# A fused attention and two-layer kernel: two PSUM banks given out as one place, and products of two steps at a time

## The chip, the cores and the metric

The kernel runs on one core of one Trainium2 chip. The metric is the device time of one execution in microseconds (us). The engines that matter are TensorE (matmuls, PE in the rows, with its weight loads as PEld), VectorE (DVE), ScalarE (ACT), GpSimd (POOL) and SyncE (SP), the last two used for issuing transfers here. Matmuls write to PSUM, which has eight banks of 512 fp32 columns for this kernel's purposes; VectorE and ScalarE read the results from there.

## What is computed

```python
def _attn_ref(x, state):                    # x (8,8,512,64), state (8,8,32,64)
    a = softmax(x @ state.T / 8);  xread = a @ state
    a2 = softmax(state @ x.T / 8); sread = a2 @ x
    return concatenate([xread, sread], axis=2)
def _moe_ref(x, w_a, w_b, w_out):           # 4352 rows, 512 -> 1536 -> 512
    return (x @ w_a) * (x @ w_b) @ w_out
def _moe2_ref(x, w_in, w_out):              # 512 -> 2048 -> 512
    h = x @ w_in
    return (h - tanh(h)) @ w_out
```

The three follow each other: attention, layer 1, layer 2. (The softmax subtracts the maximum and adds 1e-9 to the sum.)

## The kernel before

**Layer 1** goes over eight blocks of 512 tokens (blocks 0 to 7) and a block of the 256 state rows (block 8). A block has 12 steps f. In step f, `AB(blk, f)` makes two products a and b (twelve wide matmuls 128x512 of tile pab), VectorE and ScalarE form a times b in hi and lo parts (tile ph), and `X1(blk, f-1)` multiplies the step before by the output weights (twelve wide matmuls of tile acc). Every operand is kept as a hi and a lo part, and a product is made of three matmuls.

The attention read of a token block is not formed by itself: the states are multiplied with the weights first, and AB uses that product, tile mx. For blocks 0 and 1 this is `M(blk, f)`, one call a step: eight matmuls with outputs of 32x256 (16 records in the trace) into two tiles mp, one for each row half G. ScalarE writes the hi part from them; for block 0 a matmul by `minus` takes the hi part off in PSUM and ScalarE writes the lo part, for block 1 VectorE makes it. For blocks 2 to 7 it is `M_later(i, f, G)`: for blocks 2 to 5 (i = 0) 24 calls during block 1, each with twelve matmuls mq on two row tiles of 64 rows, one tile mq in PSUM for each; for blocks 6 and 7 (i = 1) 24 calls during blocks 4 and 5 on all 128 rows. These results go to memory and come back later.

Class `Att` does the attention of the next block beside that: scores (sc), transposes (pt, pl, pa), the state read (pr) and its transpose (pf). Block 0 has the attention of block 1 in it, part of its own, and also the decoding of the weights: 64-bit words come by DMA (rawab), ScalarE scales (line 116), and VectorE puts the words together in three steps (lines 119 to 121).

**PSUM before.** acc0 to acc3 are the four output tiles. In layer 1 `ab` gives out p2 and p3 in turn, and `att` gives out p0 and p1 in turn, one bank at a time, to everything else that is named above: sc, pt, pl, pa, pr, pf, mp, mq.

**Layer 2** has 64 slots with 512 tokens (`pair_slot`, eight blocks by eight slots) and eight slots with the 256 state rows (`plain_slot`). A pair slot forms the hidden layer for two feature groups from seven products of half the columns (B21, B11, T2, T3, T1, B22, T4, six narrow matmuls 128x256 each), which are added up in three tiles: y_ (py, bank p0, B21 only), x_ (px: B11, then T2, T1 and B22 on top; bank p1 in even slots and p3 in odd ones) and z_ (pz, bank p2: T3 and T4). ScalarE copies x_ after each of the four products (tile snap, lines 714, 727, 736, and h, line 748). VectorE adds the first copy to y_ (line 723, h1), others to z_ (h2). Between them stand the elementwise work of the slot before (lines 641 to 670: u, t, y, k, g) and the output matmuls acc of the slots before. In `plain_slot` a product `plain(s, g)` goes to bank p0 or p1 (g = 0, by the parity of s) or p2 or p3 (g = 1).

The order on each engine is made by the scheduler of the tile framework, which orders the instructions of the program by its own costs and puts in waits where tiles conflict. A tile is what it tracks: who reads and writes it, and when its place may be given to another tile.

## Time and profile before

| | us |
|---|---|
| median of three runs | 1451.9 |
| the three runs | 1450.9, 1451.9, 1454.3 |
| profiled execution | 1451.56 |
| its span | 1449.8 |
| TensorE busy in the span | 1427.9 (98%) |
| VectorE busy | 1129.5 (78%) |
| ScalarE busy | 904.8 (62%) |
| mean granted clock of TensorE | 0.999 |

The profile shows one execution. Busy time of an engine says how full it is, the chain that ended last says whose work set the end, and the timeline says when each instruction ran and what ended an idle time before it. Matmuls overlap: the busy time of one contains the tail in which the next is already running, so the cost of a row of matmuls is read from start to start.

### The profile page before, as it was taken

To read this page: it belongs to the slowest core of one execution; us is meant where nothing else is said; L and a number is where in the kernel's file an instruction comes from. 1 tells how busy PE (TensorE), PEld (TensorE's weight loads), DVE (VectorE), ACT (ScalarE), POOL (GpSimd) and SP (SyncE) were. 2 spreads that over 40 slices of the span, in tenths; PEclk is the share of its full clock that TensorE was granted. 3 is DMA by queue.
4 is the path that set the end of the run, shared out by engine and by line. 5 is a ranking of instruction groups with operands and counts; after the bars stand their busy time and mean duration, and the time that the engine had idled before them with its cause. 6 is when DMAs were issued, how large, how long until landed. Compare 5 with 4: busy or idle time off the path is not lost.

```text
span 1449.8 us, 23949 instructions
## 1 busy us (share of the span) xinstructions
PE 1427.9 (98%) x8928; PEld 1207.5 (83%) x8928; DVE 1129.5 (78%) x1984; ACT 904.8 (62%) x1752; POOL 207.9 (14%) x390
## 2 busy tenths in 40 slices
PE   5999999999999999999999999999999999999999
PEld 3666777878888878889988989899898998988998
DVE  6996656787544878772498988989899898988887
ACT  5765545565444556552467777777777867778675
POOL 0000001333111333320211110111101111011110
PEclk9999999999999999999999999999999999999999
DMA  8644337685546586853966667566665756656544
GB/s 297 234 144 144 130 125 220 209 265 180 163 121 183 171 255 221 249 180 126 318 195 204 197 189 224 171 205 195 204 208 174 226 171 207 204 186 211 160 146 127
DMA packets 103781, 280.50 MB, mean 193 GB/s; under 512 B 15216, under 2 KB 44400, under 8 KB 93936
## 3 DMA queue, kind: packets, MB, share of 16 engines
q0 software_dynamic: 41472, 178.28, 40.0%
q1 hardware_dynamic: 62192, 100.68, 21.2%
q8 instruction: 70, 1.15, 0.3%
q14 instruction: 47, 0.39, 0.1%
HBM read 216.53 MB, written 62.39 MB: 192 GB/s over the span
## 4 chain that ended last, share of the span: by engine, by line
PE 95%; DMA 2%; ACT 2%; DVE 1%; issue 0%; SPq 0%; ACTq 0%; DVEq 0%
PE acc L439 45%; PE pab L439 20%; PE px L630 13%; PE pz L630 6%; PE py L630 3%; PE mq L498 3%; DMA rawab<-in_wA 2%; PE mp L452 1%; PE pr L391 1%; PE sc L316 0%; PE pt L328 0%; ACT hab L116 0%; DMA x1d<-ev 0%; PE mp L460 0%; PE pa L328 0%
## 5 line engine op out<-in xcount | busy, mean ns | idle before, releaser
L439 PE MATMUL acc<-g,wo 128*128 128x512 f32 (+1 forms) x1728 | 436.1, 385 | 0.1
L439 PEld LDWEIGHTS acc<-g,wo 128*128 128x128 f32 x1728 | 293.4, 190 | 40.3 <-DVE g L670 0.3
L439 PE MATMUL acc<-ph,wo 128*128 128x512 f32 (+1 forms) x1296 | 307.7, 383 | 1.2 <-ACT ph L547 1.2
L439 PE MATMUL pab<-hl,mx 128*128 128x512 f32 x1152 | 294.7, 401 | 1.0 <-ACT hl L362 0.7
L439 PEld LDWEIGHTS acc<-ph,wo 128*128 128x128 f32 x1296 | 230.5, 188 | 53.9 <-issue 4.9
L439 PEld LDWEIGHTS pab<-hl,mx 128*128 128x128 f32 x1152 | 212.0, 189 | 62.0 <-issue 11.6
L545 DVE TENSOR_TENSOR ac<-ac,pab 128x512 f32<-128x512 f32 (+1 forms) x108 | 70.8, 656 | 142.3 <-PE pab L439 141.4
L257 POOL DMA_DIRECT2D wh<-whd x144 | 77.7, 539 | 670.3 <-PE pz L630 603.6
L665 ACT CAST g<-y 128x512 fp32r<-128x512 f32 (+1 forms) x144 | 86.0, 597 | 85.3 <-DVE y L661 84.3
L520 POOL DMA_DIRECT2D ml<-md x144 | 75.6, 526 | 421.5 <-DVE mx L526 247.5
L630 PEld LDWEIGHTS px<-T,wh 128*128 128x128 f32 x768 | 109.5, 190 | 11.0
L654 DVE SCALAR_TENSOR_TENSOR y<-y,u 128x512 f32<-128x512 f32 (+1 forms) x144 | 94.9, 659 | 26.8 <-ACT y L646 26.3
L630 PE MATMUL px<-B,wh 128*128 128x256 f32 x768 | 113.0, 283 | 1.4 <-ACT snap L736 1.4
L630 PE MATMUL pz<-T,wh 128*128 128x256 f32 x768 | 112.9, 283 | 0.0
L630 PE MATMUL px<-T,wh 128*128 128x256 f32 x768 | 112.8, 283 | 0.0
L630 PEld LDWEIGHTS px<-B,wh 128*128 128x128 f32 x768 | 105.4, 191 | 7.3 <-ACT snap L736 1.8
L542 ACT COPY ac<-pab 128x512 f32<-128x512 f32 (+1 forms) x108 | 60.7, 562 | 79.4 <-PE pab L439 79.2
L630 PEld LDWEIGHTS pz<-T,wh 128*128 128x128 f32 x768 | 105.5, 191 | 5.6
L661 DVE COPY_PREDICATED y<-k,t 128x512 f32<-128x512 int32 (+1 forms) x144 | 104.5, 726 | 2.8
L655 DVE SCALAR_TENSOR_TENSOR u<-t,u 128x512 f32<-128x512 f32 (+1 forms) x144 | 94.4, 656 | 9.0 <-ACT k L650 1.0
L670 DVE TENSOR_TENSOR g<-y,g 128x512 fp32r<-128x512 f32 (+1 forms) x144 | 94.4, 655 | 8.9 <-ACT g L665 8.8
L650 ACT ACTIVATE k<-u,consts 128x512 f32<-128x512 f32 (+1 forms) x144 | 99.8, 693 | 0.0
(233 smaller groups left out, 2089.7 us busy)
## 6 DMA issues: line engine op xcount, KB each, us to landing
wh<-whd POOLq DMA_DIRECT2D x64, 1024.0 KB, 5.3
wh<-whd POOLq DMA_DIRECT2D x72, 768.0 KB, 4.7
ml<-md POOLq DMA_DIRECT2D x144, 128.0 KB, 2.7
...
```

The lines of the kernel that those rows point to most:

```text
L257: nc.gpsimd.dma_start(t.rearrange("p a h c -> p a (h c)"), whd[j][:, a:b])
L439: nc.tensor.matmul(dst[:, cols], w[a], x[:, c, cols], start=first and i == 0, stop=last and i == 2)
L520: nc.gpsimd.dma_start(t[64 * G : 64 * G + 64, :], src[G, b])
L542: nc.scalar.copy(a[:, :n], pt[:, :n])
L545: at_v = nc.vector.tensor_tensor(a[:, :n], a[:, :n], pt[:, :n], ALU.mult)
L630: nc.tensor.matmul(dst, WP[s, piece][:, a, block(k)], XB[slots[s][0]][x][:, c, k, :], start=first and k == 0 and i == 0, stop=last and k = ...
L650: nc.scalar.activation(k, u, AF.Relu, bias=consts[:, 1:2], scale=1.0)
L654: nc.vector.scalar_tensor_tensor(y, y, PK, u, ALU.add, ALU.mult)
L655: nc.vector.scalar_tensor_tensor(u, t, C3, u, ALU.mult, ALU.mult)
L661: nc.vector.copy_predicated(y, k.bitcast(I32), t)
L665: nc.scalar.copy(GG[s, g][:, 0, : width(s)], EW[s, g][2])
L670: nc.vector.tensor_tensor(gt[:, 1, :n], EW.pop((s, g))[2], gt[:, 0, :n].bitcast(F32), ALU.subtract)
```

## The change

`att` is gone. Its two banks are one tag pp, one tile of 128 x 2 x 512, given out as a whole (`two_banks`) even where a user needs one bank (`one_bank`: pl, pa, pt, pr and pf, whose hunks are left out below). `scores` and `M` and `M_later` take both halves of one place. Attention stages are put together so that each place is emptied in the stage that fills it.

For block 1, `M_pair(blk, f)` makes steps f and f + 1 together: 16 small matmuls into two full banks, one ScalarE and one VectorE instruction of 512 columns for each row half. Its results lie in two tiles of 1024 columns, alternately in x4 and x5 and in the two mx places; a function in `MM` finds the part of a step.

In layer 2, `bank(i)` gives bank 0 and 1 as the halves of one tile PP that is taken once and kept to the end; banks 2 and 3 stay tiles of their own.

```diff
--- before.py
+++ after.py
@@ -76,7 +76,13 @@
     flat = lambda t: t.rearrange("p a b -> p (a b)")
 
 
-    att = Slots(abp, ["p0", "p1"])
+    def two_banks(name):
+
+        return abp.tile([128, 2, 512], F32, tag="pp", name=name)
+
+    def one_bank(name):
+        return two_banks(name)[:, 0]
+
     ab = Slots(abp, ["p2", "p3"])
     big = Slots(sp, [f"q{i}" for i in range(6)])
     small = Slots(sp, [f"r{i}" for i in range(8)])
@@ -187,7 +193,7 @@
                 VH[f // 2] = v_tile(f // 2, [128, 2, 1024], F32R, "wh")
             hi = VH[f // 2][:, f % 2]
         else:
-            hi = x_tile(f - 4, [128, 1024], "wh")
+            hi = x_tile(4 + (f - 6) % 4, [128, 1024], "wh")
         lo = (w_tile(2 * f - 2, [128, 1024], F32R, "wl") if f
               else big.get([128, 1024], F32R, "wl", LO0))
         nc.scalar.mul(hi, w, 2.0 ** -8)
@@ -308,8 +314,9 @@
 
         def scores(self):
 
+            sc = two_banks("sc")
             for G in range(2):
-                self.ps[G] = att.get([128, 512], F32, "sc")
+                self.ps[G] = sc[:, G]
             for p in range(KT):
                 for G in range(2):
                     r = slice(64 * G, 64 * G + 64)
...
@@ -410,15 +417,19 @@
 
             none = lambda: None
             yield none, none
-            yield none, (lambda: (self.scores(), self.load_xn()))
-            yield (lambda: (self.scale(0), self.scale(1), self.rows_max(0), self.cols_exp(0))), none
-            yield (lambda: self.cols_norm(0)), (lambda: self.turn(0))
-            yield (lambda: (self.rows_norm(0), self.turned(0))), none
+            yield none, (lambda: (self.scores(), self.load_xn(), self.scale(0), self.scale(1)))
+            yield (lambda: (self.rows_max(0), self.cols_exp(0))), none
+            if self.turned_by_pe:
+                yield (lambda: self.cols_norm(0)), none
+                yield (lambda: self.rows_norm(0)), (lambda: (self.turn(0), self.turned(0)))
+            else:
+                yield (lambda: self.cols_norm(0)), (lambda: self.turn(0))
+                yield (lambda: (self.rows_norm(0), self.turned(0))), none
             yield (lambda: (self.rows_max(1), self.cols_exp(1))), none
-            yield (lambda: self.cols_norm(1)), (lambda: self.turn(1))
-            yield (lambda: self.turned(1)), (lambda: self.sread())
-            yield (lambda: (self.sevac(), self.rows_norm(1))), (lambda: self.turn_s())
-            yield (lambda: self.keep_s()), none
+            yield (lambda: self.cols_norm(1)), (lambda: (self.turn(1), self.turned(1)))
+            yield none, (lambda: (self.sread(), self.sevac()))
+            yield (lambda: self.rows_norm(1)), (lambda: (self.turn_s(), self.keep_s()))
+            yield none, none
             yield none, none
             yield none, none
 
@@ -443,25 +454,52 @@
     minus = w_tile(23, [128, 128], F32R, "minus")
     nc.scalar.mul(minus, ident, -(2.0 ** 8))
 
+    def m_places(t):
+
+        m = t.rearrange("p a (g s c) -> p a g s c", g=2, s=2)
+        return lambda a, G, s: m[:, a, G, s, :]
+
     def M(blk, f):
 
-        mp = [att.get([128, 512], F32, "mp")[:, 0:256] for _ in range(2)]
+        both = two_banks("mp")
+        mp = [both[:, G, 0:256] for G in range(2)]
         for p in range(KT):
             for G in range(2):
                 r = slice(64 * G, 64 * G + 64)
                 nc.tensor.matmul(mp[G][32 * p : 32 * p + 32, :].rearrange("p (s c) -> p s c", s=2),
                                  STP[blk][r, 64 * p + 32 * G : 64 * p + 32 * G + 32], WA[f][r, :, p, :],
                                  start=True, stop=True)
-        m = MM[blk, f] = mix.get([128, 2, 512], F32R, "mx", *([] if blk == 0 else [MX]))
+        m = mix.get([128, 2, 512], F32R, "mx")
+        MM[blk, f] = m_places(m)
         for G in range(2):
             c = slice(256 * G, 256 * G + 256)
             nc.scalar.mul(m[:, 0, c], mp[G], 2.0 ** -8)
-            if blk == 0:
-                nc.tensor.matmul(mp[G], minus, m[:, 0, c], start=False, stop=True, skip_group_check=True)
-                nc.scalar.mul(m[:, 1, c], mp[G], 2.0 ** -8)
-            else:
-                nc.vector.scalar_tensor_tensor(m[:, 1, c], mp[G], 2.0 ** -8, m[:, 0, c].bitcast(F32),
-                                               ALU.mult, ALU.subtract)
+            nc.tensor.matmul(mp[G], minus, m[:, 0, c], start=False, stop=True, skip_group_check=True)
+            nc.scalar.mul(m[:, 1, c], mp[G], 2.0 ** -8)
+
+    def M_pair(blk, f):
+
+        both = two_banks("mp")
+        mp = [both[:, G] for G in range(2)]
+        for i in range(2):
+            for p in range(KT):
+                for G in range(2):
+                    r = slice(64 * G, 64 * G + 64)
+                    nc.tensor.matmul(
+                        mp[G][32 * p : 32 * p + 32, 256 * i : 256 * i + 256].rearrange("p (s c) -> p s c", s=2),
+                        STP[blk][r, 64 * p + 32 * G : 64 * p + 32 * G + 32], WA[f + i][r, :, p, :],
+                        start=True, stop=True, skip_group_check=True)
+        if f % 4 == 0:
+            hl = [x_tile(4 + i, [128, 1024], "mx") for i in range(2)]
+        else:
+            hl = [mix.get([128, 1024], F32R, "mx", [nm]) for nm in MX]
+        for G in range(2):
+            c = slice(512 * G, 512 * G + 512)
+            nc.scalar.mul(hl[0][:, c], mp[G], 2.0 ** -8)
+            nc.vector.scalar_tensor_tensor(hl[1][:, c], mp[G], 2.0 ** -8, hl[0][:, c].bitcast(F32),
+                                           ALU.mult, ALU.subtract)
+        for i in range(2):
+            MM[blk, f + i] = lambda a, G, s, i=i: hl[a][:, 512 * G + 256 * i + 128 * s : 512 * G + 256 * i + 128 * s + 128]
 
 
 
@@ -490,7 +528,8 @@
     def M_later(i, f, G):
         st = big.get([128, 2, 512], F32, "mst", RAW)
         tiles = [slice(0, 64), slice(64, 128)] if i == 0 else [slice(0, 128)]
-        mp = [att.get([128, 512], F32, "mq") for _ in tiles]
+        both = two_banks("mq")
+        mp = [both[:, r] for r in range(len(tiles))]
         for q in range(2):
             p = 2 * G + q
             for n, (a, c) in enumerate(hi_lo):
@@ -521,7 +560,7 @@
 
     def M_split(blk, f):
         t, m = MM[blk, f], mix.get([128, 2, 512], F32R, "mx", MX)
-        MM[blk, f] = m
+        MM[blk, f] = m_places(m)
         nc.scalar.copy(m[:, 0, :], t)
         nc.vector.tensor_tensor(m[:, 1, :], t, m[:, 0, :].bitcast(F32), ALU.subtract)
 
@@ -531,9 +570,9 @@
         for s in range(2):
             pt = ab.get([128, 512], F32, "pab")
             if blk < NB:
-                m = MM[blk, f].rearrange("p a (g s c) -> p a g s c", g=2, s=2)
+                m = MM[blk, f]
                 for G in range(2):
-                    product(pt, (m[:, 0, G, s, :], m[:, 1, G, s, :]), HL[blk][G], slice(0, n), G == 0, G == 1)
+                    product(pt, (m(0, G, s), m(1, G, s)), HL[blk][G], slice(0, n), G == 0, G == 1)
             else:
                 for k in range(KT):
                     product(pt, [w[:, s, k, :] for w in WH[f]], X0S[k], slice(0, n), k == 0, k == KT - 1)
@@ -691,7 +730,15 @@
             nc.scalar.copy(e, acc[m][:, :n])
         nc.sync.dma_start(outT[blk, m] if blk < NB else outS[m], e)
 
-    EV = [None]
+    EV, PP = [None], []
+
+    def bank(i, name):
+
+        if i < 2:
+            if not PP:
+                PP.append(two_banks("ph"))
+            return PP[0][:, i, half[0]]
+        return abp.tile([128, 512], F32, tag=f"p{i}", name=name)[:, half[0]]
 
     def OE(s, g, m):
         O(s, g, m)
@@ -700,8 +747,8 @@
     def pair_slot(s):
 
         blk, j = slots[s]
-        y_ = abp.tile([128, 512], F32, tag="p0", name="py")[:, half[0]]
-        x_ = abp.tile([128, 512], F32, tag=f"p{1 + 2 * (s % 2)}", name="px")[:, half[0]]
+        y_ = bank(0, "py")
+        x_ = bank(1 + 2 * (s % 2), "px")
         sn = mix.get([128, 3, 256], F32, "snap", SQ)
         h1, h2 = (mix.get([128, 512], F32, "h", [nm]) for nm in (mix.names[2], "ml2"))
         part(y_, s, 2, "B21", True, True)
@@ -725,7 +772,7 @@
             dve_rest(s - 1, 1)
         part(x_, s, 3, "T2", False, True)
         nc.scalar.copy(sn[:, 1], x_)
-        z_ = abp.tile([128, 512], F32, tag="p2" if s else "p0", name="pz")[:, half[0]]
+        z_ = bank(2 if s else 0, "pz")
         part(z_, s, 4, "T3", True, True)
         yield
         OE(s - 2, 1, 2)
@@ -760,7 +807,7 @@
 
     def plain(s, g):
         blk, j = slots[s]
-        t = abp.tile([128, 512], F32, tag=f"p{2 * g + s % 2}", name="ph_")[:, half[0]]
+        t = bank(2 * g + s % 2, "ph")
         x = XB[blk]
         for k in range(KT):
             w, xk = WP[s, (1, 2, 0, 7)[2 * g + k // 2]], x["B21" if k > 1 else "B11"]
@@ -826,12 +873,12 @@
             work()
 
     late0 = [
-        lambda A=A: (after_l1(lambda: (A.cols_exp(0), A.cols_norm(0))), A.turn(0)),
-        lambda A=A: (A.turned(0, tE[:, 0].rearrange("p (t s) -> p t s", s=128)),
-                     after_l1(lambda: (A.cols_exp(1), A.cols_norm(1))), A.turn(1)),
-        lambda A=A: (A.turned(1, tE[:, 1].rearrange("p (t s) -> p t s", s=128)), A.sread()),
-        lambda A=A: (A.sevac(), A.turn_s()),
-        lambda A=A: A.keep_s(),
+        lambda A=A: (after_l1(lambda: (A.cols_exp(0), A.cols_norm(0))), A.turn(0),
+                     A.turned(0, tE[:, 0].rearrange("p (t s) -> p t s", s=128))),
+        lambda A=A: (after_l1(lambda: (A.cols_exp(1), A.cols_norm(1))), A.turn(1),
+                     A.turned(1, tE[:, 1].rearrange("p (t s) -> p t s", s=128))),
+        lambda A=A: (A.sread(), A.sevac()),
+        lambda A=A: (A.turn_s(), A.keep_s()),
     ]
 
     for blk in range(NB):
@@ -892,12 +939,13 @@
                         X0S[k] = x
 
                 if nxt[0] < 2:
-                    M(*nxt)
+                    if nxt[1] % 2 == 0:
+                        M_pair(*nxt)
                 elif nxt[0] < NB:
                     M_split(*nxt)
                 AB(blk, f, bg=v, after=after)
             if blk == 0:
-                M(*nxt)
+                (M_pair if nxt[0] else M)(*nxt)
                 if f < len(late0):
                     late0[f]()
             if t and not blk:
```

TensorE, block 1, a step and a half with a group mp (M) and groups mq (M_later; wh and wl are hi and lo parts, sq the states), before:

```order
L452 MATMUL mp<-wa_457,stp 32x256 x8
L439 MATMUL pab<-hl,mx 128x512 x4
L439 MATMUL acc<-ph,wo_366 128x512 x2
L498 MATMUL mq<-wh,sq 128x256 x2
L498 MATMUL mq<-wl,sq 128x256
L498 MATMUL mq<-wh,sq 128x256 x2
L498 MATMUL mq<-wl,sq 128x256
L498 MATMUL mq<-wh,sq 128x256 x4
L498 MATMUL mq<-wl,sq 128x256 x2
L439 MATMUL acc<-ph,wo_366 128x512 x10
L498 MATMUL mq<-wh,sq 128x256 x4
```

and after, where mp stands for M_pair:

```order
L450 MATMUL acc<-ph,wo_298 128x512 x7
L488 MATMUL mp<-wa_358,stp 32x256 x8
L488 MATMUL mp<-wa_459,stp 32x256 x8
L450 MATMUL acc<-ph,wo_298 128x512 x5
L450 MATMUL pab<-hl,mx 128x512 x8
L537 MATMUL mq<-wh,sq 128x256 x4
L537 MATMUL mq<-wl,sq 128x256 x2
L537 MATMUL mq<-wh,sq 128x256 x4
L537 MATMUL mq<-wl,sq 128x256 x2
L450 MATMUL pab<-hl,mx 128x512 x4
```

The group of mq is no longer taken apart (x2, one, x2, one): its hi matmuls stand as x4, two row tiles in turn. Two steps of mp stand behind each other.

TensorE in a slot of layer 2, from B21 to T1 (py, px and pz are y_, x_ and z_), before:

```order
L630 MATMUL py<-B_8624,wh_9507 128x256 x6
L630 MATMUL px<-B_8257,wh_9507 128x256 x6
L439 MATMUL acc<-g,wo_10_6988 128x512 x6
L630 MATMUL px<-T_8862,wh_9507 128x256 x6
L630 MATMUL pz<-T_8980,wh_9507 128x256 x6
L439 MATMUL acc<-g,wo_10_6988 128x512 x3
L630 MATMUL px<-T_8743,wh_9509 128x256 x6
L439 MATMUL acc<-g,wo_10_6988 128x512 x3
L439 MATMUL acc<-g,wo_3_7002 128x512 x3
```

and after in an even slot (y_ and x_ are both ph):

```order
L669 MATMUL ph<-B_8520,wh_9627 128x256 x6
L669 MATMUL ph<-B_8157,wh_9627 128x256 x6
L450 MATMUL acc<-g,wo_12_7008 128x512 x6
L669 MATMUL pz<-T_8871,wh_9627 128x256 x6
L450 MATMUL acc<-g,wo_12_7008 128x512 x4
L669 MATMUL ph<-T_8755,wh_9627 128x256 x6
L450 MATMUL acc<-g,wo_12_7008 128x512 x2
L450 MATMUL acc<-g,wo_5_7022 128x512
L669 MATMUL ph<-T_8637,wh_9629 128x256 x6
```

T3 (pz) and four output matmuls have moved ahead of T2 (the first ph of T), which is the first to write x_ after the add of line 723 has y_ to read; T1 is the second ph of T.

VectorE in the last slots (y, u, t, k and g are the elementwise tiles; ph is the product), before:

```order
L659 SCALAR_TENSOR_TENSOR y<-y,u 128x256
L660 TENSOR_TENSOR t<-ph__15267,t 128x256
L661 COPY_PREDICATED y<-k,t 128x256
L654 SCALAR_TENSOR_TENSOR y<-y,u 128x256
L655 SCALAR_TENSOR_TENSOR u<-t,u 128x256
L670 TENSOR_TENSOR g<-y,g 128x256
L659 SCALAR_TENSOR_TENSOR y<-y,u 128x256
L660 TENSOR_TENSOR t<-ph__15314,t 128x256
L661 COPY_PREDICATED y<-k,t 128x256
L670 TENSOR_TENSOR g<-y,g 128x256
```

and after:

```order
L698 SCALAR_TENSOR_TENSOR y<-y,u 128x256
L699 TENSOR_TENSOR t<-ph,t 128x256
L700 COPY_PREDICATED y<-k,t 128x256
L699 TENSOR_TENSOR t<-ph,t 128x256
L700 COPY_PREDICATED y<-k,t 128x256
L709 TENSOR_TENSOR g<-y,g 128x256 x2
L693 SCALAR_TENSOR_TENSOR y<-y,u 128x256
L694 SCALAR_TENSOR_TENSOR u<-t,u 128x256
L698 SCALAR_TENSOR_TENSOR y<-y,u 128x256
L693 SCALAR_TENSOR_TENSOR y<-y,u 128x256
```

The work of two halves was interleaved, one t and one copy at a time; after, the two t and copies stand in a row, and the two g after them.

## Rows read from the trace of the kernel before

**Rows 1.** The page, part 4: the chain that ended last, by engine.

```profile
PE 95%; DMA 2%; ACT 2%; DVE 1%; issue 0%; SPq 0%; ACTq 0%; DVEq 0%
```

**Rows 2.** Busy time by stretch of 25 us (length, each engine, clock, DMA share, GB/s).

```profile
25.00:50.00 25.00, 23.83 (x208) 14.89 (x207) 23.70 (x40) 19.46 (x41) 0.00 (x0) 1.00 0.79 277
50.00:75.00 25.00, 23.62 (x141) 16.06 (x139) 22.46 (x38) 17.26 (x34) 0.00 (x0) 1.00 0.56 194
1000.00:1025.00 25.00, 25.00 (x158) 22.61 (x157) 23.61 (x42) 16.86 (x33) 2.69 (x5) 1.00 0.51 162
```

**Rows 3.** Timeline, TensorE, block 0 (start, busy us, instruction): M in halves and whole.

```profile
33.41 0.50 PE L439 MATMUL acc<-ph,wo 128*128 128x512 f32 x1
33.84 0.64 PE L452 MATMUL mp<-wa,stp 64*32 64x256 f32 x8
...
51.03 0.66 PE L452 MATMUL mp<-wa,stp 64*32 64x256 f32 x16
```

**Rows 4.** Timeline, TensorE, one slot of layer 2.

```profile
1073.06 0.88 PE L630 MATMUL px<-B,wh 128*128 128x256 f32 x6
1073.78 1.57 PE L439 MATMUL acc<-g,wo 128*128 128x512 f32 x6
1075.18 0.88 PE L630 MATMUL px<-T,wh 128*128 128x256 f32 x6
```

**Rows 5.** Timeline, TensorE, block 1: groups of M_later, and scores (132.11).

```profile
129.74 0.70 PE L498 MATMUL mq<-wh,sq 64*128 64x256 f32 x3
...
130.98 1.20 PE L439 MATMUL acc<-ph,wo 128*128 128x512 f32 x4
132.11 1.09 PE L316 MATMUL sc<-xTt,stp 64*32 64x512 f32 x16
...
205.64 0.50 PE L498 MATMUL mq<-wh,sq 64*128 64x256 f32 x4
...
206.32 0.28 PE L498 MATMUL mq<-wl,sq 64*128 64x256 f32 x2
206.52 1.65 PE L439 MATMUL acc<-ph,wo 128*128 128x512 f32 x6
```

**Rows 6.** Busy time from 112.8 to 231 us of line 498 (M_later) alone.

```profile
112.80:231.00 118.20, 27.65 (x288) 22.22 (x288) 1.00 0.46 148
```

**Rows 7.** Busy time from 112.8 to 231 us of line 452 (M) alone.

```profile
112.80:231.00 118.20, 9.96 (x192) 2.69 (x192) 1.00 0.46 148
```

**Rows 8.** Chain of waits, block 0 (start, us, piece): the words of the weights.

```profile
43.93 7.68 DMA rawab<-in_wA
...
51.63 1.17 ACT hab L116
```

**Rows 9.** Timeline, VectorE, block 0: the last step on the words of step 4.

```profile
46.12 1.22 DVE L121 SCALAR_TENSOR_TENSOR wa<-hab,wa 128x1024 int32<-128x1024 int32 x1
```

**Rows 10.** Timeline, TensorE, block 0: a correction by minus that waited.

```profile
54.16 0.39 PE L460 MATMUL mp<-mx,minus 128*128 128x256 f32 x1 [0.87 <-ACT mx L458]
```

**Rows 11.** Timeline, VectorE and ScalarE, same slot: the add for h1, a copy of x_.

```profile
1076.49 0.42 DVE L723 TENSOR_TENSOR h<-snap,py 128x256 f32<-128x256 f32 x1
...
1076.59 0.37 ACT L727 COPY snap<-px 128x256 f32<-128x256 f32 x1
```

**Rows 12.** Timeline, ScalarE, weight loads, TensorE: a wait in slot 1.

```profile
727.79 0.38 ACT L736 COPY snap<-px 128x256 f32<-128x256 f32 x1
...
728.22 0.78 PEld L630 LDWEIGHTS px<-B,wh 128*128 128x128 f32 x6 [1.82 <-ACT snap L736]
...
728.22 0.86 PE L630 MATMUL px<-B,wh 128*128 128x256 f32 x5 [1.39 <-ACT snap L736]
```

**Rows 13.** Timeline, VectorE, last slots.

```profile
1438.51 0.42 DVE L670 TENSOR_TENSOR g<-y,g 128x256 fp32r<-128x256 f32 x1 [0.47 <-ACT g L665]
...
1444.23 0.42 DVE L670 TENSOR_TENSOR g<-y,g 128x256 fp32r<-128x256 f32 x1 [0.47 <-ACT g L665]
```

10 lines of the change are left out of this document (5 added, 5 removed).

## The prediction, made before the changed kernel was run

> **What bounds the kernel now.** I read the chain of work that ended last first: TensorE holds 95% of it [rows 1]. So a change is worth what it takes from TensorE, or what it makes TensorE wait. The table by stage comes next [rows 2]. In block 0 (25 to 75 us) TensorE and VectorE are both nearly full, 23.83 and 23.70 of 25 us; in layer 2 TensorE leaves no gap and VectorE has 1.4 us of 25 to spare. The change touches three places: the small matmuls of blocks 0 and 1, the order inside a slot of layer 2, and the last eight slots.
>
> **Small matmuls in block 1.** Two prices matter. The first is the switch between wide and small matmuls: one wide matmul alone between two half groups takes 33.84 - 33.41 = 0.43 us [rows 3] where a row of them runs at 0.233 (1073.78 to 1075.18 is six, 1.40 us [rows 4]), so a way in and out costs 0.20 us. The second is the group itself. A half M and a whole M take nearly the same, 0.64 and 0.66 us [rows 3]: the halves run side by side only when they are issued together, so an M in halves costs about 0.57 more, and another switch. The same holds for the twelve matmuls of M_later: 1.24 us (129.74 to 130.98) from their start to the next wide one where the row tiles come one after the other, 0.88 (205.64 to 206.52) where they alternate [rows 5].
>
> By the order after, all 24 mq groups alternate (one is cut in two), and 12 M become six M_pair. Between 112.8 and 231 us the mq matmuls are busy 27.65 us and the M matmuls 9.96 [rows 6, 7]. An alternating group is busy 0.96 us (205.64 to 206.60 [rows 5]), so 24 make 23.0: 4.6 saved. For M_pair no row stands. From below it is bounded by the whole score group, with as many columns in all, 1.09 us [rows 5], from above by two whole M, 1.32 [rows 3]; I take 1.18, nearer to the score group, which has its shape, so six make 7.1: 2.9 saved. Counted in the timeline, 42 stretches of small matmuls stand between wide ones from 112.83 to 229.62; the order after has 36, and 6 x 0.20 is 1.2. Together 8.7. Busy times count the overlapping ends of matmuls too; the same sum made from intervals between starts is 45.8 us before and 37.8 after, so I take **8.0 us** saved. The evacuations that the pairs merge lie beside a full TensorE and count nothing.
>
> Against it stands the single place. With two banks given out one at a time a group could start while the one before was read; now it waits until all of that is evacuated. In the order after, 6 to 10 wide matmuls (1.4 to 2.3 us) stand between one mq group and the next, and emptying two banks is two or three instructions of 0.6 to 0.7 us on two engines, so most is covered; behind the state read and its transpose only two wide ones (0.47 us) stand ahead of the next mq. I take 1 us for such places (0 to 3): **-7.0 us**, -8 to -5.
>
> **Block 0.** Five of the M there are in halves before and none after; the scores come whole. By the same count of intervals from 22.5 to 112.8 us there are 25.4 us of small work before, and 18.9 by the order after: 6.5 less. How much of it shows is doubtful. The words of the weights come through a DMA of 7.7 us, ScalarE (1.17 us) and VectorE [rows 8], and over 25 to 75 VectorE is idle 3.8 us in all [rows 2]. On the other side, TensorE is behind there rather than ahead: M(0,4) starts at 51.03 [rows 3] and its last words were ready at 47.34 [rows 9]. And new waits appear: a whole M needs the place free from the scores, transposes and state read, and the correction by `minus` follows M at once in two places, where before one such cost 0.87 us of idle time behind ScalarE [rows 10]. I take about half, **-3.5 us** (-6.5 to 0).
>
> **Slots of layer 2.** Banks 0 and 1 are one tile there. In a slot with even number x_ lies in bank 1 and y_ in bank 0; T2 writes x_, and now waits for the VectorE add that forms h1 out of y_, though that reads the other bank. To hide it the scheduler has put T3 and four output matmuls ahead of T2. Counted from the start of the last B11 matmul (m0 = 1073.66, the sixth of those that start at 1073.06 and take 0.12 each): 0.12, six output matmuls 1.40 (1073.78 to 1075.18), T3 0.72 (as B11, 1073.06 to 1073.78), four output matmuls 0.93: T2 could start at m0 + 3.17 [rows 4]. The add is over at 1076.91 [rows 11], m0 + 3.25, and it stands in VectorE's queue behind work released before m0, so nothing brings it earlier. That is 0.08 us too late. To it comes what a wait itself costs TensorE: after its wait at 728.22 the weights are loaded 0.05 us after ScalarE ended (727.79 + 0.38), and five matmuls take as long as six in a row do, 0.86 against 0.88, so the first one costs 0.10 more [rows 4, 12]. So 0.23 us for T2. In the same slots T1 and B22 are covered by three output matmuls: 0.12 + 0.70 = 0.82 us, against 0.32 until the copy of x_ starts (estimated from its starts in the timeline), 0.37 for it [rows 11], 0.05 and 0.10: 0.02 us short each. 31 even slots x 0.27 = **+8.4 us**. Lowest 31 x 0.08 = 2.5 (the wait without its own cost), highest about 11.5 (the add 0.1 us later). Behind the waiting T2 all of TensorE's queue stands. Odd slots keep x_ in bank 3 and wait for nothing new.
>
> On PSUM the Trainium skill ("PSUM — Partial Sum Buffer", PSUM bank collisions raise a hardware error) says that engines working on different banks run clean and only a shared bank and quadrant collides. By that the chip itself would not need T2 to wait for the add, and without the wait layer 2 would lose nothing: 1442.9 us. The order with its waits shows that this program waits all the same, both banks being one tile, so I give that no more than 0.02.
>
> **The last eight slots.** The first half of a slot lies in bank 0 or 1 by parity. Because of the one tile VectorE and ScalarE take the elementwise work of two halves in pairs instead of in turn, and the next slot's first product waits for ScalarE's reading. In turn, a slot of VectorE's work takes TensorE's 5.72 us (1438.51 to 1444.23), with an idle spot of 0.47 us in it [rows 13]; the same instructions in pairs I add up to 5.85 to 5.9. So about 0.15 us a slot is lost once a slack of some 0.8 is used up, and at the end the last g comes about 1 us later with no product left to cover it. **+1.5 us** (0 to +4).
>
> **Sum.** -7.0 - 3.5 + 8.4 + 1.5 = -0.6 us. The profiled execution took 1451.56 us, 1.76 more than its span; the median is 1451.9, on which this gives **1451.3 us**: within the 0.2% (2.9 us) that a measurement can tell from no change.
>
> **Rivals.** (1) The even slots hardly wait: faster. If T2 costs only the 0.08 us by which the add is late, layer 2 loses 2.5 us and the time is 1445.4. For it: 0.08 is little, and an add 0.1 us earlier takes away all. Against it: the 0.15 us on top at 728.22. (2) The one place becomes the bound: slower. If each of some 30 hand-overs of blocks 0 and 1 leaves TensorE 0.25 us idle, because an evacuation queues behind ScalarE's 1.17 us pieces of the weights, 7.5 us go on top: 1458.8. It decides from about 0.12 us a hand-over on (+3.6 us, 1454.9). For it: both engines' queues in block 0 are full; against: 1.4 us and more of cover in block 1. (3) The change doesn't do what it says: the row tiles of a group don't run side by side when both write one tile. They would keep 1.24 us, 24 x 0.28 more than summed: 1458. The order shows them alternate into separate banks, as the group at 205.64 does, so little. (4) Block 0 gives all of its 6.5 us: 1448.3, faster.
>
> **How the numbers follow.** No change 0.41; faster 0.34 (rival 1 0.18, rival 4 and mixtures 0.14, no wait 0.02); slower 0.25 (rival 2 0.15, rival 3 0.02, the upper ends of the even slots and of the tail 0.08). 1444 to 1458 leaves out the outermost of rivals 1 and 2, about 0.1 on either side.
>
> **What would show it.** Small matmuls of block 1 in 36 stretches, mq at 0.88 us each, and block 2 some 10 us earlier than before. In layer 2 even slots of 10.9 us beside odd ones of 10.64, and T2's wait on h1 in the list of TensorE's waits, some 7 us over 31. If block 2 comes less than 6 us earlier, the hand-overs cost more than I took; if even slots take under 10.75 us, the wait is cheaper, and the kernel faster than forecast.

## The result

The changed kernel takes 1462.5 us (median of four runs, 1460.8 to 1463.1) where the kernel before takes 1452.9 on the same chip (1450.9 to 1454.3). The ratio is 1.007, with a 95% interval of 1.0056 to 1.0084: 9.6 us slower. The profiled execution took 1463.11 us, its span is 1461.3. The prediction was no change at 1451.3 us, with a range of 1444 to 1458.

The difference of the two spans is 11.5 us. It is laid out by stage below, from the starts of TensorE's matmuls in the timelines: the first wide one of AB(0,0), AB(1,0) and AB(2,1), the thirteenth (128x256 there) of AB(8,0), the start of T4 in slots 2 and 62, and the end. The columns before and after are those of the two profiled executions; the last holds the terms of the prediction's sum.

| stage | before | after | difference | predicted |
|---|---|---|---|---|
| to AB(0,0) | 21.28 | 21.61 | +0.33 | 0 |
| block 0 | 95.71 | 95.16 | -0.55 | -3.5 |
| block 1 | 116.38 | 113.93 | -2.45 | -7.0 |
| blocks 2 to 7 | 431.01 | 431.31 | +0.30 | 0 |
| block 8, slots 0 and 1 | 76.00 | 78.38 | +2.38 | 0 |
| slots 2 to 62 | 638.40 | 648.48 | +10.08 | +8.4 |
| the rest, with the last eight slots | 70.99 | 72.44 | +1.45 | +1.5 |

AB(2,1) starts 2.7 us earlier than before (230.70 for 233.37), where the prediction had named some 10, and less than 6 as the sign that the hand-overs cost more than it took.

The chain that ended last has changed, part 4 of the page of after (shares of the span):

```profile
PE 87%; DVE 6%; ACT 3%; DMA 2%; issue 1%; SPq 0%; DVEq 0%; ACTq 0%
```

TensorE held 95% of it before [rows 1] and holds 87% now; VectorE went from 1% to 6%. These are the waits in the list of TensorE's waits of after (line and tile that waited, what released it, us in total, times, longest) that are new or have grown:

```profile
PE mp L477 <- ACT mx L476: 3.8, 5, 1.4
...
PE px L669 <- ACT snap L783: 2.0, 1, 2.0
PE mq L537 <- ACT mst L542: 1.2, 3, 0.5
...
PE mp L488 <- DVE mst L544: 0.6, 2, 0.4
PE mq L537 <- DVE sm L380: 0.6, 1, 0.6
...
PE ph L669 <- DVE h L770: 0.4, 2, 0.2
```

The first is the correction by `minus` of block 0 (1.6 us in 3 before), the second slot 1 of layer 2 (1.4 before), the next three the groups of block 1. The last is T2 in the even slots of layer 2, and it has only two entries and 0.4 us, though the even slots are the largest loss of all. A slot shows why. TensorE in the even slot 34 of after (start, busy us, instruction):

```profile
1079.03 1.57 PE L450 MATMUL acc<-g,wo 128*128 128x512 f32 x6
1080.43 0.88 PE L669 MATMUL pz<-T,wh 128*128 128x256 f32 x6
1081.15 1.09 PE L450 MATMUL acc<-g,wo 128*128 128x512 f32 x4
1082.32 0.95 PE L669 MATMUL ph<-T,wh 128*128 128x256 f32 x6
1083.11 0.86 PE L450 MATMUL acc<-g,wo 128*128 128x512 f32 x3
```

Four wide output matmuls take 0.93 us [rows 4]; here T2 (ph<-T at 1082.32) starts 1.17 us after the first of them. The 0.24 us more are not idle in the profile, since the modelled end of the last wide matmul (1081.15 + 1.09 = 1082.24) covers most of them, and what is left is too short for the list. VectorE's add for h1, the weight loads of T2 and ScalarE's g in the same slot:

```profile
1081.76 0.41 DVE L770 TENSOR_TENSOR h<-snap,ph 128x256 f32<-128x256 f32 x1
...
1082.29 0.77 PEld L669 LDWEIGHTS ph<-T,wh 128*128 128x128 f32 x6 [0.47 <-ACT g L704]
...
1081.31 0.62 ACT L704 CAST g<-y 128x512 fp32r<-128x512 f32 x1 [1.01 <-DVE y L700]
```

The add ends at 1082.17, the weights are loaded from 1082.29. The view names ScalarE's g as what ended that wait, but g was done at 1081.93. Behind the add the weights follow by 0.12 us in every one of the 30 even slots from 4 to 62: T2 waits for the add, as the prediction had it. The same add stands in rows 11. The lengths of an odd and an even slot are read from T4 to T4, TensorE in after:

```profile
1086.45 0.88 PE L669 MATMUL pz<-T,wh 128*128 128x256 f32 x6
...
1097.07 0.88 PE L669 MATMUL pz<-T,wh 128*128 128x256 f32 x6
...
1108.07 0.88 PE L669 MATMUL pz<-T,wh 128*128 128x256 f32 x6
```

The odd slot takes 10.62 us and the even one 11.00; together 21.6, where two slots of before take 21.28.

### The profile page after: what moved, and what is told of

Read it like the earlier page. It is cut to its first block, busy times and chain, and to the rows that moved or that the text cites. A ratio compares the mean times of both kernels' runs of the same rounds, so it can differ in the third digit from the quotient of the medians.

```text
span 1461.3 us, 23987 instructions
## 1 busy us (share of the span) xinstructions
PE 1430.3 (98%) x8928; PEld 1191.9 (82%) x8928; DVE 1132.8 (78%) x1972; ACT 901.0 (62%) x1740; POOL 208.4 (14%) x390
## 4 chain that ended last, share of the span: by engine, by line
PE 87%; DVE 6%; ACT 3%; DMA 2%; issue 1%; SPq 0%; DVEq 0%; ACTq 0%
PE acc L450 41%; PE pab L450 19%; PE ph L669 10%; PE px L669 6%; PE pz L669 6%; PE mq L537 2%; DMA rawab<-in_wA 1%; DVE u L694 1%; DVE y L693 1%; DVE y L698 1%; PE pr L398 1%; DVE t L699 1%; DMA md<-mst 0%; DVE y L700 0%; PE pt L335 0%
## 5 line engine op out<-in xcount | busy, mean ns | idle before, releaser
L450 PE MATMUL acc<-g,wo 128*128 128x512 f32 (+1 forms) x1728 | 441.2, 385 | 0.5 <-ACT g L704 0.5
L450 PE MATMUL pab<-hl,mx 128*128 128x512 f32 x1152 | 297.7, 402 | 0.9 <-ACT hl L369 0.7
L263 POOL DMA_DIRECT2D wh<-whd x144 | 77.9, 541 | 683.0 <-PE pz L669 416.5
L693 DVE SCALAR_TENSOR_TENSOR y<-y,u 128x512 f32<-128x512 f32 (+1 forms) x144 | 94.9, 659 | 38.0 <-ACT y L685 38.0
L669 PEld LDWEIGHTS ph<-B,wh 128*128 128x128 f32 x768 | 102.6, 190 | 11.5 <-ACT snap L783 6.1
L669 PE MATMUL ph<-B,wh 128*128 128x256 f32 x768 | 108.3, 284 | 0.0
L685 ACT ACTIVATE y<-u,consts 128x512 f32<-128x512 f32 (+1 forms) x144 | 98.8, 686 | 0.7 <-DVE g L709 0.6
L698 DVE SCALAR_TENSOR_TENSOR y<-y,u 128x512 f32<-128x512 f32 (+1 forms) x144 | 95.0, 660 | 2.7
```

Source lines behind the costliest of these rows:

```text
L263: nc.gpsimd.dma_start(t.rearrange("p a h c -> p a (h c)"), whd[j][:, a:b])
L450: nc.tensor.matmul(dst[:, cols], w[a], x[:, c, cols], start=first and i == 0, stop=last and i == 2)
L669: nc.tensor.matmul(dst, WP[s, piece][:, a, block(k)], XB[slots[s][0]][x][:, c, k, :], start=first and k == 0 and i == 0, stop=last and k = ...
L685: nc.scalar.activation(y, u, AF.Square, bias=consts[:, 0:1], scale=1.0)
L693: nc.vector.scalar_tensor_tensor(y, y, PK, u, ALU.add, ALU.mult)
L698: nc.vector.scalar_tensor_tensor(y, y, PC, u, ALU.add, ALU.mult)
```

## The experiments

Each is compared with the kernel before on the same chip, whose medians were 1453.1, 1453.1, 1453.5 and 1452.9 us in four sets of runs. A table behind them has the stages of all profiles. Of the edits the deciding lines are shown; `...` marks what is left out.

### Layer 2 apart

y_ goes alone into a place that is taken anew each slot, x_ always into bank 3, and the last eight slots' first products into places of their own.

```diff
...
-            return PP[0][:, i, half[0]]
+            return one_bank(name)[:, half[0]]
...
-        y_ = bank(0, "py")
-        x_ = bank(1 + 2 * (s % 2), "px")
+        y_ = bank(0, "py") if s else first()[:, 0, half[0]]
+        x_ = bank(3, "px") if s else first()[:, 1, half[0]]
...
```

> The change with layer 1 as it is, but in layer 2 y_ alone in the place pp and x_ in bank 3 in every slot but slot 0, and the last slots' first product alone in pp: no tile there holds two things any more. Theory (the tie between the two banks costs layer 2 its loss): slots of 10.64 us again, even ones too, so about 10 us off the pair slots and 1.4 off the end: a span near 1449.8 us and a time of 1450 to 1452 us. Rival (the even slots grow for another reason, such as the order of ScalarE's work or where layer 1 leaves the transfers): even slots stay above 10.9 us and the time stays at 1459 or more.

Measured: 1450.5 us, ratio 0.9986 (0.9974 to 0.9997). Slots 2 to 62 take 638.40 us again, to the hundredth what they took before. So the tie of y_ and x_ is the whole loss of the pair slots; layer 1 of the change, still in this kernel, is worth a little. T4 in two slots that follow each other, T2 and the add:

```profile
1079.13 0.88 PE L669 MATMUL pz<-T,wh 128*128 128x256 f32 x6
...
1089.77 0.88 PE L669 MATMUL pz<-T,wh 128*128 128x256 f32 x6
...
1073.45 0.88 PE L669 MATMUL px<-T,wh 128*128 128x256 f32 x6
...
1074.77 0.40 DVE L773 TENSOR_TENSOR h<-snap,py 128x256 f32<-128x256 f32 x1
```

Here, as in the kernel before, T2 is over before the add begins (1074.33 and 1074.77), and while the add reads y_ (in the kernel before from 1076.49 to 1076.91 [rows 11]) TensorE goes on writing T3 and output matmuls into other banks, at no cost that shows. That agrees with the Trainium skill ("PSUM — Partial Sum Buffer", PSUM bank collisions raise a hardware error), which has accesses to different banks run clean. The wait was the program's, not the chip's.

### The last eight slots tied again

The same, but the first products of the last eight slots are again halves of one tile.

```diff
...
-        t = bank(2 * g + s % 2, "ph")
+        t = tied()[:, s % 2, half[0]] if g == 0 else bank(2 + s % 2, "ph")
```

> Layer 2 apart in the pair slots, but the first products of the last eight slots are again the halves of one tile, as in the change. Theory: the end alone costs 1 to 2 us, so 1451.5 to 1452.5 us where the run with all apart had 1450.5. Rival (the end costs nothing, TensorE has work to cover it): 1450 to 1451 us.

Measured: 1452.1 us, 1.5 more than the run with all apart (1450.5, in another set, in which the kernel before had the same median). That alone is not clear of the spread of these two sets (1449.8 to 1453.9, and 1447.4 to 1456.7). The profiles are clearer: the rest behind slot 62 takes 72.44 and 72.47 us in the two kernels that tie the last slots, and 70.98 to 71.55 in the twelve others, 71.42 in the run with all apart. VectorE's first g of a slot and TensorE's last output matmuls in the change show how:

```profile
1443.49 0.41 DVE L709 TENSOR_TENSOR g<-y,g 128x256 fp32r<-128x256 f32 x1
...
1449.33 0.42 DVE L709 TENSOR_TENSOR g<-y,g 128x256 fp32r<-128x256 f32 x1
...
1453.85 3.61 PE L450 MATMUL acc<-g,wo 128*128 128x256 f32 x24 [0.48 <-ACT g L704]
```

From 1443.49 to 1449.33 is 5.84 us, where a slot took 5.72 [rows 13]; and at 1453.85 TensorE has stood still for 0.48 us until ScalarE's g was there.

### Two tiles in layer 1

M_pair and the regrouped attention stages stay, but p0 and p1 are two tiles given out in turn, in both layers.

```diff
+    att = Slots(abp, ["p0", "p1"])
     def two_banks(name):
-        return abp.tile([128, 2, 512], F32, tag="pp", name=name)
+        return [att.get([128, 512], F32, name) for _ in range(2)]
     def one_bank(name):
-        return two_banks(name)[:, 0]
+        return att.get([128, 512], F32, name)
...
-        both = two_banks("mq")
-        mp = [both[:, r] for r in range(len(tiles))]
+        mp = [one_bank("mq") for _ in tiles]
...
```

> The change with M_pair and the regrouped attention stages, but p0 and p1 as two tiles given out in turn, in layer 1 and in layer 2. Theory (in layer 1 the gain was lost because the two banks of one tile are emptied one after the other): the copies of a group of M_later on ScalarE and VectorE may start together again, the waits of TensorE in block 1 (about 4.4 us beyond the switches) mostly go, although some groups fall apart into unpaired ones; the second AB of block 2 begins 5 to 6 us earlier than in the kernel before and the time is 1445 to 1448 us. Rival (a group waits because it needs both banks, not because of the order of emptying): nothing gained in block 1 over the change, 1449 to 1451 us.

Measured: 1451.1 us, ratio 0.9984 (0.9975 to 0.9992), so less than expected. From here on the wait in front of a small group is read from starts: as a rule the next start comes 0.33 us after that of the wide matmul ahead of the group, and what goes beyond is counted as a wait. These waits are gone in block 1 as expected, 0.7 us where the change has 4.0. But the mq matmuls come in 116 pieces of one kind (hi or lo parts), where 24 alternating groups make 96, and the row halves of three M_pairs come partly one after the other (the five of block 1 take 6.6 us from start to start, 5.1 in the change). By the same count of intervals as in the prediction, small work with its switches and waits takes 42.3 us of block 1 here and 40.3 in the change. Block 1 takes 114.50 us, no better than with one tile (113.93, where the change loses another 1.2 us among its wide matmuls, see the pairs in a row below). The expectation had counted the waits and not the fragments that come in their place.

### Copies in a row

The second of the two copies that empty a group of M_later waits for the first.

```diff
...
+            if r:
+                tc.add_manual_dep(copies[1].ins, copies[0].ins.name, mybir.DependencyInfo(
+                    mybir.DependencyClass.Sync, mybir.DependencyReason.DATA))
...
```

> The same with one wait added: of the two copies that empty a group of M_later the second waits for the first. Theory: this alone gives back 2 to 4 us of what the run with two tiles gains, since the next group starts some 0.6 us later at most of the 24 hand-overs and part of that is covered. Rival: within 0.7 us of the run with two tiles, since wide matmuls cover the copies either way.

Measured: 1452.7 us, 1.6 more than with two tiles, and block 1 takes 116.94, 2.4 more. It looked like the theory's number. But TensorE's waits have not come back (0.2 us for M_later in the list): the order is another one. The mq matmuls still come in 116 pieces, but the row halves of each M_pair of block 1 now come partly one after the other, 8.5 us from start to start for 6.6, and small work takes 44.9 us for 42.3. So this run can't tell emptying in turn from another order, and a run that keeps the order was needed (below).

### Pairs only

The kernel before with M_pair alone.

```diff
...
-                    M(*nxt)
+                    if nxt[1] % 2 == 0:
+                        M_pair(*nxt)
...
```

> The kernel before with M_pair for block 1 alone, everything else as it was. Theory: six groups of 1.02 us and a switch take the place of twelve M and their halves, 12 x 0.79 + 1.5 - 6 x 1.23 = 3.6 us off, some of it lost to more unpaired groups of M_later: 1448 to 1450 us, faster. Rival (the pairs need both banks longer and push M_later's groups apart): no change, 1451 to 1453 us.

Measured: 1451.0 us, ratio 0.9983 (0.9973 to 0.9993). Block 1 takes 115.69, 0.7 less than before, and not 3.6: M_pair costs 1.02 us as priced where it stays together, but two of the five in block 1 take longer (1.21 and 1.80), and the mq matmuls go up to 27.1 us from start to start, 1.3 more than before, in 124 pieces for 118. And more than the 0.7 is lost in slot 1 (78.68 for 76.00).

### The output copies of block 8

Slot 1 had shown a wait of ScalarE for a store. ScalarE in slot 1 of after, and the stretch from 725 to 730 us there (length, busy time of PE, PEld, DVE, ACT, POOL, granted clock of TensorE, DMA share, GB/s):

```profile
726.00 0.37 ACT L609 COPY ev<-acc 128x256 f32<-128x256 f32 x1 [3.03 <-DMA x1d<-ev]
726.27 0.38 ACT L783 COPY snap<-px 128x256 f32<-128x256 f32 x1
...
725.00:730.00 5.00, 3.30 (x14) 3.02 (x15) 2.83 (x6) 3.57 (x8) 0.00 (x0) 0.71 0.80 271
```

The same of before:

```profile
727.52 0.37 ACT L570 COPY ev<-acc 128x256 f32<-128x256 f32 x1 [2.42 <-DMA x1d<-ev]
...
725.00:730.00 5.00, 3.61 (x25) 3.00 (x24) 3.78 (x9) 2.52 (x7) 0.54 (x1) 1.00 1.01 328
```

The copy `ev` is one of four that bring the last outputs of layer 1 from acc to a place from which they are stored; the third needs the place of the first, whose store is in flight among the weight loads for layer 2 (DMA share 0.80 to 1.01). Behind it on ScalarE stands the copy of x_, and B22 waits for that [rows 12]. In after it comes 1.5 us earlier than in before, though block 8 began 2.4 us earlier. And the granted clock is 0.71 there, where it is 1.00 before. So the copies got four places, the halves of two tiles.

```diff
                 if blk == NB:
-                    e = big.get([128, 512], F32, "ev", RAW)
+                    if m % 2 == 0:
+                        ev2 = big.get([128, 2, 512], F32, "ev", RAW)
+                    e = ev2[:, m % 2]
```

> The kernel before, with the four output copies of the state rows at the end of layer 1 in the halves of two places, so that the third no longer waits until the first has been stored. Theory (slot 1 of layer 2 waits on that store while the transfers are full, so what layer 1 gains ahead of it is given back there): TensorE's wait of 1.5 us in slot 1 goes and the time falls by 1 to 2.5 us, to about 1451. Rival (the next transfer is late as well and takes its place): 1453, no change.

Measured, in the kernel before: 1450.2 us, ratio 0.9978 (0.9969 to 0.9987). The wait in slot 1 is gone, and block 8 with slots 0 and 1 takes 74.38 us for 76.00. That is 1.6 of the 2.9 us by which the medians differ; where the others lie is not shown.

> The run with layer 2 apart, with the same change of the output copies. Theory: without the wait in slot 1, and without the lower granted clock behind it, the 2.4 us that layer 1 gains reach the end, and slot 2 comes 4 us or more earlier than in the kernel before: 1447.5 to 1449.5 us. Rival: slot 2 stays within 2 us of the kernel before, and the time at 1450.5.

Measured, with layer 2 apart: 1448.9 us, ratio 0.9967 (0.9957 to 0.9978). The stage takes 74.59 us for 78.31, 3.7 less, and in the same stretch the clock is 1.00:

```profile
725.00:730.00 5.00, 5.00 (x33) 4.28 (x32) 4.93 (x11) 3.53 (x8) 1.07 (x2) 1.00 1.06 368
```

The medians fell only by 1.6, and in the two profiles nothing arrives at the end (spans of 1448.5 and 1448.4), since block 0 took 96.50 us here, 3.4 more than in the run with layer 2 apart, from the same code. What happened there stands below, under block 0.

### The whole place in two tiles

To separate the whole place from the emptying in turn, the two tiles are kept, and the first matmul of a group of M_later or of an M_pair waits for the readers of the group before it, on both banks (with the new output copies too).

```diff
...
+    EMPTY = []
+    def after_emptied(first, emptied):
+        for i in EMPTY:
+            tc.add_manual_dep(first.ins, i.ins.name, mybir.DependencyInfo(
+                mybir.DependencyClass.Sync, mybir.DependencyReason.DATA))
+        EMPTY[:] = emptied
...
+        after_emptied(mms[0], read)
...
```

> Two tiles again, with the changed output copies, and each group of M_later and each M_pair waits until both banks of the one before it are emptied: the place is given out as a whole, but its two banks are emptied side by side. Theory (emptying in turn is what costs block 1 its waits): TensorE's waits between groups in block 1, 4.4 us beyond the switches with one tile, fall to 2 us or less while 21 of 24 groups still alternate; block 1 is 2 us shorter than with one tile and the time 1445 to 1447.5 us. Rival (one place is too few, however it is emptied): waits of 3.5 us or more remain, and the time is that of the run with layer 2 apart and the changed copies, within 0.7 us.

Measured: 1446.3 us, ratio 0.9956 (0.9942 to 0.9969). The time is as expected, the reason only in part: the waits between groups are down from 4.5 to 0.8 us, but block 1 takes 113.64 us, only 0.7 less than with one tile in the run before it, since groups behind the scores, transposes and state read still stand in fragments (112 pieces). Half of what the profiled span is shorter than in that run (1444.4 for 1448.4) lies in block 0 (94.46 for 96.50).

> As the run with the whole place in two tiles, and now a group of M_later or an M_pair also waits until the scores, transposes and state read ahead of it are emptied. All but two groups of M_later in block 1 alternate, as with one tile. Theory (with one tile the loss is the emptying in turn): the small matmuls of block 1 come down to the amount of the change, and the waits between groups stay near 1 us where one tile had 4.4: block 1 another 2 to 3 us shorter than in the run before it, 1443 to 1445 us. Rival (a place given out whole costs waits however it is emptied): the fragments turn into waits of the same length, 1446 to 1447 us as before.

Here these readers are waited for as well (`EMPTY.append` around the copies of the scores, transposes, state read and its transpose). Measured: 1445.3 us, ratio 0.9946 (0.9933 to 0.9958); block 1 takes 112.44 us, 1.2 less than in the run before it and about 1.5 to 1.9 less than with one tile. The mq matmuls come in 106 pieces, and the waits are 1.7 us. So with more of the change's order kept, two tiles are better than one in block 1.

> The same with one wait added: of the two copies of each group of M_later the second waits for the first, as with one tile. Theory: the waits between groups come back, 2 to 4 us, and the time is 1446 to 1448 us. Rival: no more than 0.7 us behind the run without it.

The added wait is that of "copies in a row". Measured: 1444.9 us, ratio 0.9942 (0.9928 to 0.9956), the fastest kernel of the study, and block 1 takes 112.24, with waits of 2.0 us and 100 pieces. The theory fell here: where it had 2 to 4 us of waits come back, they rise by 0.3. That the run isn't slower at all is owed to the order, which is not quite the same (six pieces fewer, 1.1 us of mq from start to start).

> The run with the copies of M_later in a row, and now the two halves of an M_pair are emptied in a row as well (ScalarE begins the second when VectorE is done with the first). Theory (M_pair's emptying in turn is what block 1 waits for with one tile): six hand-overs longer by 0.5 us or so, 1 to 2.5 us more, 1446 to 1447.5 us. Rival (covered like the copies of M_later): within 0.7 us of 1445.

```diff
-            nc.scalar.mul(hl[0][:, c], mp[G], 2.0 ** -8)
+            hi = nc.scalar.mul(hl[0][:, c], mp[G], 2.0 ** -8)
+            if G:
+                tc.add_manual_dep(hi.ins, read[0].ins.name, mybir.DependencyInfo(
+                    mybir.DependencyClass.Sync, mybir.DependencyReason.DATA))
```

Measured: 1447.3 us, ratio 0.9964 (0.995 to 0.9978), 2.4 us more than the run before it; block 1 takes 114.37, 2.1 more and about what one tile takes. The mq pieces are again 100. The waits between groups rise from 2.0 to 3.4 us. So it is M_pair that loses by emptying in turn. An M_pair in the change, TensorE, ScalarE and VectorE (line 488, 498, 499), and a weight load of the AB behind it:

```profile
149.69 1.09 PE L488 MATMUL mp<-wa,stp 64*32 64x256 f32 x32
...
150.90 0.60 ACT L498 ACTIVATE mx<-mp 128x512 fp32r<-128x512 f32 x1 [2.82 <-PE mp L488]
152.25 0.60 ACT L498 ACTIVATE mx<-mp 128x512 fp32r<-128x512 f32 x1 [0.76 <-DVE mx L499]
...
151.53 0.69 DVE L499 SCALAR_TENSOR_TENSOR mx<-mp,mx 128x512 fp32r<-128x512 f32 x1 [2.07 <-ACT mx L498]
152.88 0.69 DVE L499 SCALAR_TENSOR_TENSOR mx<-mp,mx 128x512 fp32r<-128x512 f32 x1 [0.66 <-ACT mx L498]
...
152.90 0.76 PEld L450 LDWEIGHTS pab<-hl,mx 128*128 128x128 f32 x4 [0.25 <-ACT mx L498]
```

Four readers, one after the other, from 150.90 to 153.57. The same in the run before this one (two tiles, all readers waited for, copies of M_later in a row):

```profile
163.23 1.10 PE L499 MATMUL mp<-wa,stp 64*32 64x256 f32 x32 [0.33 <-DVE mst L557]
...
164.41 1.09 ACT L509 ACTIVATE mx<-mp 128x512 fp32r<-128x512 f32 x2 [2.05 <-PE mp L499]
...
165.47 1.28 DVE L510 SCALAR_TENSOR_TENSOR mx<-mp,mx 128x512 fp32r<-128x512 f32 x2
```

Both of ScalarE's follow at once (164.41 to 165.50) and both of VectorE's too; the place is empty 2.34 us after the first began, not 2.67, and ScalarE is done with it after 1.09 us, not 1.95. That costs in two ways. The next group waits longer for the place: 1.4 of the 2.1 us. And AB, which reads what M_pair's readers write (tile mx), waits for it: the weight load at 152.90 follows ScalarE's second copy, which ended at 152.85. By starts, wide matmuls of block 1 that follow a wide one come more than 0.27 us after it in one place in the run before (0.1 us beyond the pace), in seven with the pairs in a row (0.75 us), and in ten in the change (1.2 us, of which 0.7 in eight places behind an M_pair). The list doesn't show these waits, but for one of 0.2 us.

> The same, and now scores, transposes and state read of block 1 take the whole place too: each waits until both banks of the one before are emptied, and the next group waits for them. With this the two tiles behave in block 1 as the one tile does. Theory (the whole place for users that need one bank is what costs): another 1 to 2 us, block 1 at 114 us as with one tile, 1447 to 1448 us. Rival: within 0.7 us of the run before it; then what is left between one tile and two lies in block 0 or in the order of the other engines.

Here scores, transposes, state read and its transpose take the whole place too, by the same `after_emptied`. Measured: 1446.3 us, ratio 0.9957 (0.9944 to 0.9969), block 1 at 113.44, waits 2.3 us. The further loss of the theory isn't there. At 1.0 us less than the run before it, it lies outside the rival's 0.7 too, on the fast side; why isn't settled.

### The stages of all runs

In us, from the profiled executions, as in the table of the result; the last column is the median of the timed runs.

| run | block 0 | block 1 | block 8, slots 0, 1 | slots 2 to 62 | rest | median |
|---|---|---|---|---|---|---|
| before | 95.71 | 116.38 | 76.00 | 638.40 | 70.99 | 1452.9 |
| the change | 95.16 | 113.93 | 78.38 | 648.48 | 72.44 | 1462.5 |
| layer 2 apart | 93.08 | 113.99 | 78.31 | 638.40 | 71.42 | 1450.5 |
| last eight slots tied | 92.87 | 114.25 | 76.13 | 638.40 | 72.47 | 1452.1 |
| two tiles | 93.80 | 114.50 | 77.88 | 638.40 | 71.02 | 1451.1 |
| copies in a row | 94.30 | 116.94 | 76.09 | 638.49 | 71.00 | 1452.7 |
| pairs only | 93.64 | 115.69 | 78.68 | 638.40 | 71.23 | 1451.0 |
| before, output copies | 94.96 | 116.37 | 74.38 | 638.59 | 70.98 | 1450.2 |
| layer 2 apart, output copies | 96.50 | 114.35 | 74.59 | 638.52 | 71.41 | 1448.9 |
| whole place in two tiles | 94.46 | 113.64 | 74.37 | 638.40 | 71.00 | 1446.3 |
| all readers waited for | 93.86 | 112.44 | 74.39 | 638.65 | 70.99 | 1445.3 |
| that, copies in a row | 93.67 | 112.24 | 74.39 | 638.40 | 71.54 | 1444.9 |
| that, pairs in a row | 94.16 | 114.37 | 74.33 | 638.38 | 71.55 | 1447.3 |
| that, every user whole | 93.41 | 113.44 | 74.39 | 638.53 | 71.21 | 1446.3 |

## Why the prediction was wrong

Four terms were too favourable: the hand-overs in block 1, the half of block 0's saving that was to show, a further loss in slot 1 that the sum left out, and, by less, the even slots.

**Block 1: the hand-over term failed.** The work was priced well: mq groups 0.88 to 0.90 us from start to start (0.88 predicted), M_pair busy 1.09 (I took 1.18), 36 stretches as counted. (The stretches of the kernel before are 40 by the trace and not 42; the 8.0 us come from the intervals and don't use that.) The step that failed is "I take 1 us for such places (0 to 3)". By the starts of matmuls the groups of the change wait 4.0 us beyond the usual switch, and those of before 0.2. One such wait in the change, before an M_pair, TensorE, ScalarE and VectorE:

```profile
168.92 1.10 PE L488 MATMUL mp<-wa,stp 64*32 64x256 f32 x32 [0.40 <-DVE mst L544]
...
167.57 0.57 ACT L542 COPY mst<-mq 128x512 f32<-128x512 f32 x1
...
168.17 0.69 DVE L544 COPY mst<-mq 128x512 f32<-128x512 f32 x1 [0.24 <-ACT mst L542]
```

The two copies of the group before it stand one behind the other (167.57, 168.17), the second on another engine, though they read different banks, and TensorE resumes at 168.92. I had put the emptying at two or three instructions on two engines; an M_pair has four, and with one tile all readers of the place go in turn. The second thing that I left out is the waiting inside AB, 1.2 us, most of it for M_pair's results. Of the 4.55 us that block 1 misses (2.45 for 7.0) the waits between groups beyond the 1 us taken make 2.8, and AB 1.2. By part: emptying in turn costs 0.3 us of waits for M_later's copies and about 2 us in all for M_pair's readers. Even the best run misses the -7 by 2.9 (112.24 is -4.1); it still has 2.0 us of waits and four pieces more than the 96. Which hand-overs the waits that are left belong to was not tried apart.

**Block 0: half was too much.** I took half of 6.5 us. From start to start the small matmuls of block 0 take 24.0 us before and 20.7 in the change, but the block is only 0.55 us shorter. The four profiles with the change's code in block 0 have 95.16, 93.08, 96.50 and 92.87 us, a mean of 94.4; the ten with two tiles lie from 93.41 to 95.71, with a mean of 94.2. So on average nothing shows, and the same code varies by 3.6 us between executions. One wait parts the four. In the change, TensorE and ScalarE:

```profile
62.72 0.66 PE L469 MATMUL mp<-wa,stp 64*32 64x256 f32 x16
...
65.68 0.39 PE L477 MATMUL mp<-mx,minus 128*128 128x256 f32 x1 [1.40 <-ACT mx L476]
...
64.21 1.15 ACT L122 ACTIVATE hab<-rawab 128x1024 f32<-128x1024 f32 x1 [1.97 <-DMA rawab<-in_wA]
65.27 0.36 ACT L476 ACTIVATE mx<-mp 128x256 fp32r<-128x256 f32 x1
```

M begins at 62.72 and is over in 0.6 us, but its first reader on ScalarE (line 476, at 65.27) stands behind the scaling of the weights, and that waited 1.97 us for their transfer. `minus` waits with it, 1.40 us. The run with 96.50 has the same wait:

```profile
65.56 0.39 PE L477 MATMUL mp<-mx,minus 128*128 128x256 f32 x1 [1.74 <-ACT mx L476]
...
65.00:70.00 5.00, 4.44 (x16) 3.51 (x17) 2.48 (x4) 3.39 (x9) 0.00 (x0) 0.70 0.77 288
```

Its granted clock is 0.70 from 65 to 70 us, where it is 1.00 in the three others. In the two short ones (93.08 and 92.87) ScalarE waited 0 and 0.39 us for that transfer, and the wait of `minus` is not there; they are shorter than all ten with two tiles. So what block 0 gains is lost where that transfer comes late. How much of the gain is the whole M's was not tried apart. The row of VectorE that I read as TensorE being behind [rows 9] was no evidence that TensorE would gain.

**Slot 1: not in the sum.** The prediction had [rows 12] open, and used them only for the price of a wait. What ends that wait is a store, in a stretch in which the transfers are full. Block 8 began 2.4 us earlier and slot 2 came no earlier (T4 at 740.40 for 740.38). Of the 2.38 us of the stage 0.6 is the longer wait (2.0 for 1.4). The rest is about what the lower granted clock takes: 0.71 and 0.95 over two stretches of 5 us are 1.7 us less at full clock, an estimate. As the runs with the new output copies show, the stage can be 3.7 shorter in all (78.31 to 74.59), of which 1.6 were there before. This is the step that was missing: for each place that gets faster, to ask for the next wait that is set by something else. But the gain isn't lost there each time: in the run with the last eight slots tied, block 8 began 3.0 us earlier than before, TensorE waited 1.3 us, the clock stayed at 1.00, and the stage took 76.13.

**Even slots: the mechanism right, the term too small.** T2 waits for the add in each even slot and nowhere else, and taking the tie away takes all of it away. The term was 0.27 us for each even slot and measured 0.34 (10.98 for 10.64 in the settled slots; odd ones are 0.02 shorter). By the slot above: the add is late by 0.09 (I had 0.08), T2 begins 0.15 behind it (0.05), its first matmul takes 0.07 us more than usual (0.10), T1 and B22 lose 0.03 (0.04). So the mis-sized part is the time from release to start: I took 0.05 us from a wait for ScalarE [rows 12]; after VectorE's add the weight load alone takes 0.12. The stage is 1.7 us over its term, of the 11 us that the forecast missed.

**Where I looked for it was wrong.** I said that the list of waits would show some 7 us for T2. It shows 0.4. The evidence is in the spacing of starts.

**The last eight slots: right.** +1.45 in the profile of the change for +1.5; the tie alone is 1.05 in the profiles, against the run with all apart.

**The rivals.** The second, the one place as the bound, was given 0.15. It had 0.25 us for each of 30 hand-overs, 7.5 in all, and the two blocks fell 7.5 short of their terms (3.0 against 10.5). That the sums agree is luck: the groups of block 1 wait 0.11 us each (4.0 over 35), the rest is AB's waiting and a late transfer in block 0. Rivals 1, 3 and 4 did not come. The range failed since its bounds were made of single terms, while all errors lay on one side: block 1, block 0, slot 1 and the even slots together are 11.6 us.
